# Expert weight sums: 64 jobs spread over three stages instead of two, with other buffers and other DMA rows

## The chip, the cores and the metric

The kernel runs on one core of a Trainium2 chip. The metric is the time of one execution on the device in microseconds (us): 1686.47 us before the change, the median of 3 runs (1685.59 to 1688.97). The engines are named as in the profile: PE (TensorE matmuls), PEld (its weight loads), DVE (VectorE), ACT (ScalarE), POOL (GpSimd) and SP (SyncE, whose queue issues almost all DMAs here).

## What is computed

The reference, cut to its three stages (S = 768, 2 batches, 8 heads of 64, 8 experts):

```
q_assign, k_assign = argmax of the normalised q, k against 16 centroids
scores = scale * q @ k.T, kept where q_assign == k_assign, else -1e9
x = softmax(scores) @ v                       # attention, 1536 x 512
h = x @ w_in; g = max(h, 0) + log1p(exp(-|h|))
x = g @ w_out                                 # first feed-forward stage, d_ff = 2048
P = softmax-like gate, 8 rounds of row and column normalisation
for e in range(8):
    out += P[:, e:e+1] * (relu(x @ w1[e]) @ w2[e])   # d_ff = 1024 per expert
```

## The kernel before

All matmuls take fp32 operands as two parts, a rounded one (names with h) and the rest (names with l), and make three products: h·h, h·l, l·h. A "split" is what makes the two: ACT casts, and POOL or DVE subtracts.

**Attention** (0 to 335 us): 8 head pairs, each of 4 halves of 6 steps, 192 steps in all. Scores go through line 478 (`s`), exponentials through ACT (`E`, line 491), transposes through PE (`t`, line 518), their split `eh`/`el` (lines 521 and 525), and the products with v through line 533 (`av`). All is put into a list of events with a step number, the list is sorted, and the pieces of code are recorded in that order; then a scheduler sets each engine's own order.

**First feed-forward stage** (335 to 656 us): 16 units (8 column blocks fc times 2 token blocks) of 48 first-layer matmuls (line 637, `p`) and 48 second-layer matmuls (`y`). The weights come as 64-bit numbers: `fetch_unit` loads them (SP, lines 133 and 137) and `to32` converts them on ACT and DVE (lines 117 to 121, `cm`, `wf`, `w2f`) once for two units; `split_unit` then splits them on ACT and POOL (lines 231 to 236, `wlA`, `wlBD`, `w2l`). The conversions of the next fc write `wf` (one buffer) and `w2f` (three tiles, two for each fc), which the splits of this fc read.

**Expert stage** (656 to 1685 us): 16 passes (8 experts times 2 token blocks) of 28 steps. Each pass multiplies 2 x 2 blocks with seven products instead of eight, so it needs sums of weight blocks, T1 to T4, of w1 and of w2. In a pass, 4 units u of 7 first-layer groups (line 887) use w1 parts A, B, C (`w1_load`, `w1_split`, lines 814 and 815: `whAm`, `wlAm`, `wlCm` and so on), and 14 second-layer pieces (line 922) use w2 parts (`w2_load`, line 835 and on, `w2_split`, lines 844 and 845: `vh`, `vl`; `vl` is made on POOL, three pieces ahead of its use). `vl` and `wlC` are POOL's whole work there.

**The weight sums** are made ahead of time, in 64 jobs (m = 0 for w1 or 1 for w2, expert e, quarter u):
- `t_load` (lines 188 and 191): SP loads 512 KB into a tile `ts`;
- `t_sums` (line 200): four subtractions 128x256 on POOL, in place;
- `t_store` (line 203): SP writes the tile's 512 KB into DRAM (`td`). `w1_load` (parts B and C) and `w2_load` read it from there in the expert stage.

A tile `ts` is free when its store has landed. The 32 w2 jobs run in attention with 3 tiles, the 32 w1 jobs in the first feed-forward stage with 2 tiles; the expert stage has none. The two loops that set when each part of a job is recorded:

```
t = 24 + 4.9 * n                # attention steps: load t, sums t + 6, store t + 12
divmod(int(3.2 * m) + o, 7)     # feed-forward slots (7 per unit): o = 0, 3, 5
```

Of the kernel before, what the change touches and what calls it, by code (L numbers as in the profile page):

```python
# [20 lines left out]
def attention_moe_moe2(ctx, tc, v, qt, kt, centroids, w_in, w_out, w_gate, w1, w2, eye, out, dbg=None):  # L21
# [139 lines left out]
    def fetch_unit(u):  # L161
# [11 lines left out]
            [lambda c=c: conv_half(w2f[c], r2, "2", c) for c in range(2)],  # L173
        )

    TD = [
        [[tc.dram_tile([P, 4, KC // 2 * P], F32, name=f"td{m}_{e}_{u}") for u in range(NF2)] for e in range(E)]
        for m in range(2)
    ]
    TS = {}  # L180
    TORD = (("T1", "T3", "T2", "T4"), ("T1", "T3", "T4", "T2"))

    def t_load(pool, m, e, u):
        t = TS[m, e, u] = slot_pool[pool].tile([P, 4, KC // 2 * P], F32, tag="ts", name=f"ts{m}_{e}_{u}", bufs=TSB[pool])
        for fh in range(2):
            o = fh * (FE // 2) + u * P
            if m:
                nc.sync.dma_start(t[:, 2 * fh : 2 * fh + 2, :].rearrange("p s d -> p (s d)"), w2[e, o : o + P, :])
            else:
                for j in range(2):  # L190
                    nc.sync.dma_start(
                        t[:, (0, 3, 1, 2)[2 * fh + j], :].rearrange("p (k f) -> p k f", f=P),
                        w1[e, j * DM // 2 : (j + 1) * DM // 2, o : o + P].rearrange("(k p) f -> p k f", p=P),
                    )

    def t_sums(m, e, u):
        t = TS[m, e, u]
        b11, b12, b22, b21 = (t[:, n, :] for n in ((0, 1, 3, 2) if m else (0, 1, 2, 3)))
        for o_, u_, v_ in ((b11, b12, b11), (b12, b22, b12), (b22, b22, b11), (b21, b21, b22)):
            nc.gpsimd.tensor_tensor(o_, u_, v_, ALU.subtract)  # L200

    def t_store(m, e, u):
        nc.sync.dma_start(TD[m][e][u], TS.pop((m, e, u)))

    TSB = {"ap": 3, "fp": 2}

    WT = {}

# [10 lines left out]
    def split_unit(u):  # L219
        nm = f"{u[0]}{u[1]}_{u[2]}_{u[3]}"  # L220
        par = u[3] % 2
        w2f = W[u]
        T = {"A": w1_tiles("A", par, nm), "D": w1_tiles("B", par, "D" + nm, "fp" if par else "mp")}
        w2h, w2l = (slot_pool["fp"].tile([P, 2, DM], F32R, tag=f"w2{t}{par}", name=f"w2{t}" + nm, bufs=1) for t in "hl")
        W[u] = w1_use(T), w2h, w2l

        def w1_(ch):
            h, l = T[ch]
            o = SLOT[MEMBERS[ch][0]]
            src = wf[:, o : o + 2, :]  # L230
# [348 lines left out]
        at(92 + (n - 1) * 1.36, lambda n=n: fetch_first(n), ("fu", 0))  # L579
    for n in range(4):  # L580
        at(175 + n * 5, lambda n=n: x_split("1_0", first_blk, n), ("xs", 0))
    for n in range(E * NF2):
        e, u = divmod(n, NF2)
        t = 24 + 4.9 * n
        at(t, lambda e=e, u=u: t_load("ap", 1, e, u), ("tl", 0))
        at(t + 6, lambda e=e, u=u: t_sums(1, e, u), ("tq", 0))
        at(t + 12, lambda e=e, u=u: t_store(1, e, u), ("tw", 0))
    KEEP = {'sp2': 1, 'fr': 0, 'av': 1, 'am3': 1, 'tpa': 1, 'smc': 0, 'm0': 1, 'rw': 1, 'pz': 1, 'e1': 1}
    events.sort(key=lambda x: x[:2])
    last_prep = max(key for key, _, fn, _ in events if fn in prep_fns)  # L590
# [194 lines left out]
    def w1_load(k, u, ch):  # L785
        e = k % E
        if ch == "A" and u % 2 == 0:
            for c_, b_ in CHUNK.items():
                WR[0, c_] = [wf[:, b_ : b_ + (3 if c_ == "C" else 2), :]]
        dst = WR[u % 2, ch]  # L790
        if ch == "A":
            nc.sync.dma_start(
                dst[0].rearrange("p s (k f) -> p (s k) f", f=P),
                w1[e, :, u * P : (u + 1) * P].rearrange("(k p) f -> p k f", p=P),
            )
        elif ch == "B":
            nc.sync.dma_start(dst[0], TD[0][e][u][:, 0:4:2, :])
        else:
            o = FE // 2 + u * P
            b22 = dst[0][:, 0, :]  # L800
            nc.sync.dma_start(
                b22.rearrange("p (k f) -> p k f", f=P),
                w1[e, DM // 2 : DM, o : o + P].rearrange("(k p) f -> p k f", p=P),
            )
            nc.sync.dma_start(dst[0][:, 1:3, :] if len(dst) == 1 else dst[1], TD[0][e][u][:, 1:4:2, :])

    def w1_split(k, u, ch):
        par = u % 2 if ch == "A" else 0
        h, l = T = w1_tiles(ch, par, f"m{k}_{u}")
        n = 0  # L810
        for src in WR[u % 2, ch]:
            m = src.shape[1]
            hs = h[:, n : n + m, :]
            nc.scalar.copy(hs, src)  # L814
            (nc.gpsimd if ch == "C" else nc.vector).tensor_tensor(l[:, n : n + m, :], src, hs.bitcast(F32), ALU.subtract)
            n += m
        W1U.setdefault((k, u), {}).update(w1_use({ch: T}))

# [22 lines left out]
    def w2_split(k, i, p):
        src = W2R[(7 * k + i) % 4][:, 2 * p : 2 * p + 2, :]
# [139 lines left out]
    for k in range(NB):  # L982
# [123 lines left out]
```

## Time and profile before

| what | value |
|---|---|
| median of 3 runs | 1686.47 us (1685.59 to 1688.97) |
| the profiled execution | 1686.74 us, its span 1684.9 us |
| mean granted TensorE clock, share of full speed | 0.961 |
| busy: PE, PEld, DVE, ACT, POOL | 1556.9, 1472.5, 1266.4, 1006.4, 830.8 us |
| sums `ts` on POOL (line 200) | 256 instructions, 203.5 us busy, 798 ns each |
| splits `vl` on POOL (line 845) | 224 instructions, 356.9 us busy, 1594 ns each |
| store of a job, from issue to landing, median | 3.1 us (512 KB) |

The busy times are sums over stages that have different limits, so the stage is what to look at first, and within it the waits and the timelines. A group of rows below is cited by its number. In a row of waits the engine and line on the left waited for what stands on the right. A time in square brackets in a timeline is the idle time ahead of the row, and what ended it.

### The profile page before, as it was taken

The page shows a single profiled execution, that of the slowest core. Times are in us where ns is not written, and L with a number is a line of the kernel's source. Part 1 is how long each engine was busy: PE and PEld are TensorE (multiplying, and loading weights), DVE is VectorE, ACT ScalarE, POOL GpSimd, SP SyncE. Part 2 cuts the span into 40 slices and gives each one's busy share as a digit, 9 for nine tenths or more (in the row PEclk, how much of TensorE's full clock was granted, in tenths as well). Part 3 has the DMA queues.
Part 4 walks back from the last instruction along what each step waited for, and adds up shares of the span by engine and source line. Part 5 has one row for each costly group of instructions (what it writes and reads, how often), then busy time and mean ns, then how long its engine had stood idle before and what let it go on. Part 6 is the DMA issues. An engine that isn't in the chain of part 4 may idle for free. (4 is left out here: it accounts for less than half of the span.)

```text
span 1684.9 us, 27842 instructions
## 1 busy us (share of the span) xinstructions
PE 1556.9 (92%) x9873; PEld 1472.5 (87%) x9873; DVE 1266.4 (75%) x1835; ACT 1006.4 (60%) x1854; POOL 830.8 (49%) x728
## 2 busy tenths in 40 slices
PE   5888898779777998999999999998999999999998
PEld 4777777668777997789999999998999999999998
DVE  4997877696555636697788787889687878877867
ACT  4777777655444554555666656656566656666654
POOL 3465656586555412234554445446444444544444
PEclk7989989899979999999999999999999999999999
DMA  8667877367666410233333444343534343443321
GB/s 219 174 188 218 235 241 217 129 185 230 213 200 194 147 32 26 91 99 118 119 120 117 125 127 125 112 124 94 166 118 125 113 126 123 122 124 118 121 72 65
DMA packets 228090, 236.30 MB, mean 140 GB/s; under 512 B 16880, under 2 KB 199280, under 8 KB 227952
## 3 DMA queue, kind: packets, MB, share of 16 engines
q1 hardware_dynamic: 227808, 234.47, 45.5%
q8 instruction: 77, 1.26, 0.3%
q14 instruction: 61, 0.50, 0.1%
q10 hardware_dynamic: 144, 0.07, 0.0%
HBM read 177.32 MB, written 36.70 MB: 127 GB/s over the span
## 5 line engine op out<-in xcount | busy, mean ns | idle before, releaser
L845 POOL TENSOR_TENSOR vl<-w2r,vh 128x512 fp32r<-128x512 f32 x224 | 356.9, 1594 | 459.1 <-ACT vh L844 413.9
L200 POOL TENSOR_TENSOR ts<-ts 128x256 f32<-128x256 f32 x256 | 203.5, 798 | 113.9 <-DMA ts<-in_moe_w_dram 83.6
L866 DVE TENSOR_TENSOR gl<-XA,gh 128x768 fp32r<-128x768 f32 x160 | 168.1, 1051 | 86.3 <-ACT gh L865 86.3
L865 ACT CAST gh<-XA 128x768 fp32r<-128x768 f32 x160 | 133.9, 837 | 114.6 <-PE Ya1m L922 97.6
L922 PE MATMUL Ya0m<-vh,gl 128*128 128x256 f32 x512 | 144.7, 283 | 0.0
L922 PE MATMUL Ya0m<-vl,gh 128*128 128x256 f32 x512 | 144.6, 282 | 0.0
L922 PE MATMUL Ya0m<-vh,gh 128*128 128x256 f32 x512 | 144.5, 282 | 0.0
L844 ACT CAST vh<-w2r 128x512 fp32r<-128x512 f32 x224 | 137.6, 615 | 9.2 <-PE y L671 5.9
L525 DVE TENSOR_TENSOR el<-t,eh 128x384 fp32r<-128x384 f32 x192 | 102.4, 551 | 33.4 <-ACT eh L521 32.3
L486 DVE TENSOR_REDUCE sc<-s 128x1 f32<-128x768 f32 x96 | 91.3, 952 | 28.4 <-PE s L478 27.8
L922 PE MATMUL Yb0m<-vl,gh 128*128 128x256 f32 x384 | 109.6, 285 | 2.5 <-POOL vl L845 2.5
L922 PE MATMUL Yb0m<-vh,gh 128*128 128x256 f32 x384 | 109.3, 285 | 2.3 <-DVE x L940 2.3
L922 PE MATMUL Yb0m<-vh,gl 128*128 128x256 f32 x384 | 109.7, 286 | 1.9 <-DVE gl L866 1.9
L521 ACT CAST eh<-t 128x384 fp32r<-128x384 f32 x192 | 90.0, 481 | 34.5 <-PE t L518 28.6
L518 PE MATMUL t<-idf,E 128*128 128x128 f32 x576 | 103.7, 293 | 6.9 <-ACT E L491 3.3
L491 ACT ACTIVATE E<-s,sc 128x768 f32<-128x768 f32 x96 | 86.9, 905 | 30.9 <-DVE sc L486 27.2
L908 ACT ACTIVATE XA<-XA 128x768 f32<-128x768 f32 x96 | 81.1, 844 | 28.8 <-DVE XA L906 28.7
L922 PEld LDWEIGHTS Ya0m<-vh,gl 128*128 128x128 f32 x512 | 97.5, 190 | 0.0
L922 PEld LDWEIGHTS Ya0m<-vh,gh 128*128 128x128 f32 x512 | 97.4, 190 | 0.0
L922 PEld LDWEIGHTS Ya0m<-vl,gh 128*128 128x128 f32 x512 | 97.3, 190 | 0.0
L518 PEld LDWEIGHTS t<-idf,E 128*128 128x128 f32 x576 | 78.0, 151 | 19.1 <-DVE el L525 7.5
L860 DVE TENSOR_TENSOR XS<-XA,XA 128x768 f32<-128x768 f32 x32 | 64.6, 2020 | 33.6 <-ACT XA L904 33.6
(243 smaller groups left out, 5334.2 us busy)
## 6 DMA issues: line engine op xcount, KB each, us to landing
td<-ts SPq DMA_DIRECT2D x64, 512.0 KB, 3.1
w2r<-td SPq DMA_DIRECT2D x256, 128.0 KB, 2.5
w2r<-in_moe_w_dram SPq DMA_DIRECT2D x48, 512.0 KB, 3.7
ts<-in_moe_w_dram SPq DMA_DIRECT2D x64, 256.0 KB, 4.4
ts<-in_moe_w_dram SPq DMA_DIRECT2D x128, 128.0 KB, 3.7
wf<-td SPq DMA_DIRECT2D x64, 256.0 KB, 3.2
w1r<-td SPq DMA_DIRECT2D x64, 256.0 KB, 3.1
AT<-HL SPq DMA_DIRECT2D x64, 192.0 KB, 5.3
```

Of the source, the lines that this page charges most:

```text
L200: nc.gpsimd.tensor_tensor(o_, u_, v_, ALU.subtract)
L486: nc.vector.tensor_reduce(SC[i][:, 0, j, t : t + 1], Et[i, t][:, :, 0:CB], AX.XY, ALU.max, negate=True)
L491: nc.scalar.activation(e.rearrange("p (a c) -> p a c", a=2), Et[i, t][:, :, 0:CB], AF.Exp, bias=sc[:, 0, j, t : t + 1], scale=1.0, accum_o ...
L518: nc.tensor.transpose(pt[:, t * P : (t + 1) * P], Et[i, t][:, s * P : (s + 1) * P], idf)
L521: nc.scalar.copy(eh, TT[i, s])
L525: nc.vector.tensor_tensor(el, TT.pop((i, s)), EHL[i, s].bitcast(F32), ALU.subtract)
L844: nc.scalar.copy(h, src)
L845: nc.gpsimd.tensor_tensor(l, src, h.bitcast(F32), ALU.subtract)
L865: nc.scalar.copy(h, src)
L866: nc.vector.tensor_tensor(l, src, h.bitcast(F32), ALU.subtract)
L908: nc.scalar.activation(t, t, AF.Relu)
L922: nc.tensor.matmul(ps, g[:, v, ts], w[:, v, :], start=i in (0, 1, 3) and p == 0 and v == 0 and n == 0 and t != 1, stop=p == 1 and v == 1 a ...
```

## The change

The same 64 jobs are made in another order (by expert: w1 then w2 of expert 0, and so on) and in three places: 16 jobs (experts 0 and 1) in attention, one each 10 steps, with load, sums and store 0, 8 and 17 steps after its start, 3 tiles; 24 (experts 2 to 4) in the first feed-forward stage, one each 3.9 slots, 0, 5 and 10 slots, 4 tiles; 24 (experts 5 to 7) in the expert stage, recorded one each 7 steps, at 0, 3 and 5.5 steps, with 1 tile. A job is cut in another way for w1 (128 rows of the matrix and 512 of its columns), so its loads are 2 DMAs of 256 KB in rows of 1 KB (4 of 128 KB in rows of 512 B before), and for w2 they are 2 of 256 KB in rows of 2 KB. Stores write rows of 1 KB (4 KB before), as one DMA of 512 KB (w2) or two of 256 KB (w1). A w2 part of sums now comes back with one DMA of 512 KB (4 of 128 KB), the sums in parts B and C of w1 in rows of 512 B (1 KB). Part A of w1 has one pair of tiles in the expert stage instead of two; in the feed-forward stage the odd pair moves to another pool. Every sum, split and matmul is there as often as before.

```diff
     TD = [
-        [[tc.dram_tile([P, 4, KC // 2 * P], F32, name=f"td{m}_{e}_{u}") for u in range(NF2)] for e in range(E)]
-        for m in range(2)
+        [tc.dram_tile([4, 2, P, HF], F32, name=f"td0_{e}") for e in range(E)],
+        [tc.dram_tile([4, NF2, P, DM // 2], F32, name=f"td1_{e}") for e in range(E)],
     ]
     def t_load(pool, m, e, u):
...
+        for h in range(2):
             if m:
-                nc.sync.dma_start(t[:, 2 * fh : 2 * fh + 2, :].rearrange("p s d -> p (s d)"), w2[e, o : o + P, :])
+                o = h * HF + u * P
+                src, d = w2[e, o : o + P, :].rearrange("p (s d) -> p s d", s=2), t[:, 2 * h : 2 * h + 2, :]
             else:
-                for j in range(2):
-                    nc.sync.dma_start(
-                        t[:, (0, 3, 1, 2)[2 * fh + j], :].rearrange("p (k f) -> p k f", f=P),
-                        w1[e, j * DM // 2 : (j + 1) * DM // 2, o : o + P].rearrange("(k p) f -> p k f", p=P),
-                    )
+                k, c = divmod(u, 2)
+                o = h * DM // 2 + k * P
+                src = w1[e, o : o + P, :].rearrange("p (s f) -> p s f", s=2)[:, :, c * 256 : (c + 1) * 256]
+                d = t[:, 2 * h : 2 * h + 2, :]
+            nc.sync.dma_start(d, src)
     def t_store(m, e, u):
-        nc.sync.dma_start(TD[m][e][u], TS.pop((m, e, u)))
-
-    TSB = {"ap": 3, "fp": 2}
+        t = TS.pop((m, e, u))
+        if m:
+            nc.sync.dma_start(TD[1][e][:, u].rearrange("s p d -> p s d"), t)
+            return
...
+        for n, ts_ in enumerate((t[:, 0:4:3, :], t[:, 1:3, :])):
+            nc.sync.dma_start(TD[0][e][2 * n : 2 * n + 2, k, :, cs].rearrange("s p f -> p s f"), ts_)
+
+    TSB = {"ap": 3, "fp": 4, "gp": 1}
+    JOBS = [(m, e, u) for e in range(E) for m in range(2) for u in range(NF2)]
+    JA, JF = 4 * NF2, 10 * NF2
-        T = {"A": w1_tiles("A", par, nm), "D": w1_tiles("B", par, "D" + nm, "fp" if par else "mp")}
+        pool = "fp" if par else "mp"
+        T = {"A": w1_tiles("A", par, nm, pool), "D": w1_tiles("B", par, "D" + nm, pool)}
-    for n in range(E * NF2):
-        e, u = divmod(n, NF2)
-        t = 24 + 4.9 * n
-        at(t, lambda e=e, u=u: t_load("ap", 1, e, u), ("tl", 0))
-        at(t + 6, lambda e=e, u=u: t_sums(1, e, u), ("tq", 0))
-        at(t + 12, lambda e=e, u=u: t_store(1, e, u), ("tw", 0))
+    for n, job in enumerate(JOBS[:JA]):
+        t = 22 + 10 * n
+        for o, fn, c_ in ((0, t_load, "tl"), (8, t_sums, "tq"), (17, t_store, "tw")):
+            at(t + o, lambda fn=fn, job=job: fn(*((("ap",) if fn is t_load else ()) + job)), (c_, 0))
     def w1_split(k, u, ch):
-        par = u % 2 if ch == "A" else 0
-        h, l = T = w1_tiles(ch, par, f"m{k}_{u}")
+        h, l = T = w1_tiles(ch, 0, f"m{k}_{u}")
     def w2_load(k, i):
...
-            n = TORD[1].index(name)
-            for u in range(NF2):
-                nc.sync.dma_start(dst[:, u, :], TD[1][e][u][:, n, :])
+            nc.sync.dma_start(dst, TD[1][e][TORD.index(name)].rearrange("u p d -> p u d"))
+    for n, job in enumerate(JOBS[JF:]):
+        t = G1 + 7 * n + 1.5
+        do(t, t_load, "gp", *job)
+        do(t + 3, t_sums, *job)
+        do(t + 5.5, t_store, *job)
-    for m in range(E * NF2):
-        e, u = divmod(m, NF2)
-        for o, fn in ((0, lambda e=e, u=u: t_load("fp", 0, e, u)), (3, lambda e=e, u=u: t_sums(0, e, u)),
-                      (5, lambda e=e, u=u: t_store(0, e, u))):
-            tsum_at.setdefault(divmod(int(3.2 * m) + o, 7), []).append(fn)
+    for n, job in enumerate(JOBS[JA:JF]):
+        for o, fn in ((0, lambda job=job: t_load("fp", *job)), (5, lambda job=job: t_sums(*job)),
+                      (10, lambda job=job: t_store(*job))):
+            tsum_at.setdefault(divmod(int(3.9 * n) + o, 7), []).append(fn)
```

Three places show what this does to the order. The line numbers of the change are some 11 to 16 higher than before (478 becomes 489, 518 becomes 529, 533 becomes 544).

PE in attention, third pair. Before, the score products of halves 10 and 11 (`s10_1` to `s11_1`, lines 478) stand in a row behind a transpose, with no transpose and no product with v between them:

```order
L518 MATMUL t8_5_1445<-idf_65,E8_2_1318 128x128
L478 MATMUL s10_1_1473<-AT210_736,AT200_690 128x384 x2
L478 MATMUL s10_1_1473<-Bt210_737,Bt200_691 128x384 x2
L478 MATMUL s10_2_1513<-AT210_736,AT200_690 128x384 x2
L478 MATMUL s10_2_1513<-Bt210_737,Bt200_691 128x384 x2
L478 MATMUL s11_0_1557<-AT211_741,AT201_695 128x384 x2
L478 MATMUL s11_0_1557<-Bt211_742,Bt201_696 128x384 x2
L478 MATMUL s11_1_1592<-AT211_741,AT201_695 128x384 x2
L478 MATMUL s11_1_1592<-Bt211_742,Bt201_696 128x384 x2
```

The change, at the same transpose:

```order
L529 MATMUL t8_5_1383<-idf_65,E8_2_1255 128x128
L544 MATMUL av8_1322<-eh8_3_1344,VV20_851 128x384
L489 MATMUL s10_1_1408<-AT210_688,AT200_642 128x384 x2
L544 MATMUL av8_1322<-el8_3_1346,VV20_851 128x384
L529 MATMUL t9_0_1398<-idf_65,E9_0_1290 128x128
L529 MATMUL t9_0_1398<-idf_65,E9_1_1331 128x128
L529 MATMUL t9_0_1398<-idf_65,E9_2_1374 128x128
L544 MATMUL av8_1322<-eh8_4_1360,VV20_851 128x384
L489 MATMUL s10_1_1408<-Bt210_689,Bt200_643 128x384
```

The scores are now one or two at a time between transposes and products with v. Such runs stand at four places before (at `s10_1`, `s14_1`, `s18_1`, `s22_1`), and the change has none of the four; a shorter one at `s6_2` is in both.

SP in the first feed-forward stage (`ts0_2_2` is the tile of w1, expert 2, quarter 2; `td` its store, `r110` and `r210` raw weights). Before, two loads, then the two stores of the same jobs:

```order
L191 DMA ts0_2_2_5067<-in_moe2_w1_dram 128x2x128 x4
L191 DMA ts0_2_3_5146<-in_moe2_w1_dram 128x2x128 x4
L133 DMA r110_0_4_5306<-in_moe_w_in_dram 128x4x128
L203 DMA td0_2_2_84<-ts0_2_2_5067 128x1024
L203 DMA td0_2_3_85<-ts0_2_3_5146 128x1024
L137 DMA r210_0_4_5307<-in_moe_w_out_dram 128x512
L191 DMA ts0_3_0_5203<-in_moe2_w1_dram 128x2x128 x4
L191 DMA ts0_3_1_5284<-in_moe2_w1_dram 128x2x128 x4
```

The change:

```order
L195 DMA ts0_3_0_4828<-in_moe2_w1_dram 128x2x256 x2
L206 DMA td1_2_84<-ts1_2_2_4630 128x4x256
L195 DMA ts0_3_1_4939<-in_moe2_w1_dram 128x2x256 x2
L206 DMA td1_2_84<-ts1_2_3_4715 128x4x256
L195 DMA ts0_3_2_5028<-in_moe2_w1_dram 128x2x256 x2
L211 DMA td0_3_77<-ts0_3_0_4828 128x2x256 x2
```

Each store is now preceded by the load of the job two places later.

POOL in the expert stage, passes 2 and 3 (`vl2_10` is the split of piece 1, half 0, in pass 2; `ts` the sums). Before, the same splits stand there without the sums. The change:

```order
L857 TENSOR_TENSOR vl2_00_8743<-w2r1_6919,vh2_00_8742 128x512
L857 TENSOR_TENSOR vl2_01_8798<-w2r1_6919,vh2_01_8797 128x512
L201 TENSOR_TENSOR ts0_7_1_10618<-ts0_7_1_10618 128x256 x4
L857 TENSOR_TENSOR vl2_10_8851<-w2r1_6919,vh2_10_8850 128x512
L829 TENSOR_TENSOR wlCm3_0_8899<-wf_71,whCm3_0_8898 128x768
L857 TENSOR_TENSOR vl2_11_8903<-w2r1_6919,vh2_11_8902 128x512
L201 TENSOR_TENSOR ts0_7_2_10801<-ts0_7_2_10801 128x256 x4
L857 TENSOR_TENSOR vl2_20_8956<-w2r0_6918,vh2_20_8955 128x512
```

All 24 jobs stand between the first splits of pass 0 and `wlCm3_3`, the last part of w1 in pass 3: some 7 in a pass, though they were recorded 4 in a pass.

## Rows read from the trace of the kernel before

**Rows 1.** Windows: us, PE, PEld, DVE, ACT, POOL busy, clock, DMA share, GB/s.
```profile
0.00:335.00 335.00, 274.43 (x1555) 237.42 (x1556) 254.20 (x453) 226.21 (x493) 183.79 (x243) 0.90 0.69 203
335.00:572.00 237.00, 194.79 (x1006) 179.35 (x1006) 156.35 (x223) 116.63 (x232) 145.60 (x154) 0.90 0.64 201
...
797.00:1100.00 303.00, 303.00 (x2098) 299.59 (x2097) 241.44 (x313) 190.03 (x320) 148.33 (x100) 1.00 0.39 121
```

**Rows 2.** Windows, matmuls of line 637 alone: us, PE, PEld busy, clock, DMA, GB/s.
```profile
347.10:554.50 207.40, 94.24 (x432) 83.88 (x433) 0.88 0.67 209
414.30:432.70 18.40, 9.26 (x49) 8.15 (x49) 1.00 0.84 256
371.50:392.20 20.70, 10.44 (x49) 9.31 (x50) 0.92 0.69 213
...
572.40:655.90 83.50, 45.30 (x240) 40.93 (x240) 1.00 0.14 43
```

**Rows 3.** Waits of SP's queue, 340 to 560 us: total us, times, longest.
```profile
SPq L203 <- POOL ts L200: 92.9, 28, 6.4
```

**Rows 4.** Waits of the other engines, 380 to 560 us, same columns.
```profile
POOL ts L200 <- DMA ts<-in_moe_w_dram: 55.1, 12, 8.4
...
PE p L637 <- DVE gf L651: 29.9, 10, 7.0
...
DVE w2f L119 <- POOL w2l L236: 19.8, 3, 8.9
```

**Rows 5.** Timeline of SP's queue: start, us, operation; no wait is in brackets here.
```profile
435.18 3.77 SPq L203 DMA_DIRECT2D td<-ts  x2
439.00 0.43 SPq L133 DMA_DIRECT2D r<-in_moe_w_in_dram  x1
439.47 4.64 SPq L191 DMA_DIRECT2D ts<-in_moe_w_dram  x8
```

**Rows 6.** Timeline of POOL: start, us, operation, idle before and releaser.
```profile
431.76 6.82 POOL L200 TENSOR_TENSOR ts<-ts 128x256 f32<-128x256 f32 x8 [7.04 <-DMA ts<-in_moe_w_dram]
...
445.20 6.88 POOL L200 TENSOR_TENSOR ts<-ts 128x256 f32<-128x256 f32 x8 [4.12 <-issue]
...
459.72 3.15 POOL L200 TENSOR_TENSOR ts<-ts 128x256 f32<-128x256 f32 x4 [6.38 <-DMA ts<-in_moe_w_dram]
```

**Rows 7.** Timeline of PE in attention, at the run of scores `s10_1`.
```profile
111.53 0.62 PE L478 MATMUL s<-AT,AT 128*128 128x384 f32 x2 [1.03 <-ACT E L491]
...
112.94 0.62 PE L478 MATMUL s<-AT,AT 128*128 128x384 f32 x2 [0.43 <-ACT E L491]
...
114.58 0.62 PE L478 MATMUL s<-AT,AT 128*128 128x384 f32 x2 [0.68 <-ACT E L491]
...
117.56 0.69 PE L533 MATMUL av<-el,VV 128*128 128x384 f32 x1 [1.40 <-DVE el L525]
```

**Rows 8.** Waits of PE, 264 to 331 us, end of attention.
```profile
PE rb L512 <- POOL rw L49: 6.1, 2, 4.5
```

**Rows 9.** Timeline of POOL in the expert stage.
```profile
678.13 2.50 POOL L845 TENSOR_TENSOR vl<-w2r,vh 128x512 fp32r<-128x512 f32 x2 [2.56 <-ACT vh L844]
...
832.51 1.99 POOL L815 TENSOR_TENSOR wlCm<-w1r,whCm 128x256 fp32r<-128x256 f32 x2
...
893.21 1.99 POOL L815 TENSOR_TENSOR wlCm<-w1r,whCm 128x256 fp32r<-128x256 f32 x2
```

**Rows 10.** DMA issues in attention, 0 to 335 us: count, KB, median us to landing.
```profile
ts<-in_moe_w_dram SPq DMA_DIRECT2D x64, 256.0 KB, 4.4
td<-ts SPq DMA_DIRECT2D x32, 512.0 KB, 4.1
```

**Rows 11.** DMA issues in the feed-forward stage, 380 to 560 us.
```profile
td<-ts SPq DMA_DIRECT2D x25, 512.0 KB, 3.0
```

**Rows 12.** DMA issues in the expert stage, 800 to 1100 us.
```profile
w1r<-in_moe_w_dram SPq DMA_DIRECT2D x10, 256.0 KB, 3.8
wf<-in_moe_w_dram SPq DMA_DIRECT2D x10, 256.0 KB, 2.8
```

More of the change, by code (lines that the diff above doesn't have):

```diff
@@ L174, in fetch_unit @@
         )
+    HF = FE // 2
     TD = [
-        [[tc.dram_tile([P, 4, KC // 2 * P], F32, name=f"td{m}_{e}_{u}") for u in range(NF2)] for e in range(E)]
-        for m in range(2)
+        [tc.dram_tile([4, 2, P, HF], F32, name=f"td0_{e}") for e in range(E)],
+        [tc.dram_tile([4, NF2, P, DM // 2], F32, name=f"td1_{e}") for e in range(E)],
     ]
     TS = {}
-    TORD = (("T1", "T3", "T2", "T4"), ("T1", "T3", "T4", "T2"))
+    TORD = ("T1", "T3", "T4", "T2")
     def t_load(pool, m, e, u):
-        t = TS[m, e, u] = slot_pool[pool].tile([P, 4, KC // 2 * P], F32, tag="ts", name=f"ts{m}_{e}_{u}", bufs=TSB[pool])
-        for fh in range(2):
-            o = fh * (FE // 2) + u * P
+        t = TS[m, e, u] = slot_pool[pool].tile([P, 4, 256], F32, tag="ts", name=f"ts{m}_{e}_{u}", bufs=TSB[pool])
+        for h in range(2):
             if m:
-                nc.sync.dma_start(t[:, 2 * fh : 2 * fh + 2, :].rearrange("p s d -> p (s d)"), w2[e, o : o + P, :])
-            else:
-                for j in range(2):
-                    nc.sync.dma_start(
-                        t[:, (0, 3, 1, 2)[2 * fh + j], :].rearrange("p (k f) -> p k f", f=P),
-                        w1[e, j * DM // 2 : (j + 1) * DM // 2, o : o + P].rearrange("(k p) f -> p k f", p=P),
-                    )
+                o = h * HF + u * P
+                src, d = w2[e, o : o + P, :].rearrange("p (s d) -> p s d", s=2), t[:, 2 * h : 2 * h + 2, :]
+            else:
+                k, c = divmod(u, 2)
[3 more added lines that the diff above has]
+            nc.sync.dma_start(d, src)
     def t_sums(m, e, u):
         t = TS[m, e, u]
-        b11, b12, b22, b21 = (t[:, n, :] for n in ((0, 1, 3, 2) if m else (0, 1, 2, 3)))
+        b11, b12, b21, b22 = (t[:, n, :] for n in range(4))
         for o_, u_, v_ in ((b11, b12, b11), (b12, b22, b12), (b22, b22, b11), (b21, b21, b22)):
@@ L202, in t_store @@
     def t_store(m, e, u):
-        nc.sync.dma_start(TD[m][e][u], TS.pop((m, e, u)))
-    TSB = {"ap": 3, "fp": 2}
+        t = TS.pop((m, e, u))
+        if m:
+            nc.sync.dma_start(TD[1][e][:, u].rearrange("s p d -> p s d"), t)
+            return
+        k, c = divmod(u, 2)
+        cs = slice(c * 256, (c + 1) * 256)
+        for n, ts_ in enumerate((t[:, 0:4:3, :], t[:, 1:3, :])):
[3 more added lines that the diff above has]
+    JA, JF = 4 * NF2, 10 * NF2
     WT = {}
@@ L796, in w1_load @@
         elif ch == "B":
-            nc.sync.dma_start(dst[0], TD[0][e][u][:, 0:4:2, :])
+            nc.sync.dma_start(
+                dst[0].rearrange("p s (k f) -> p (s k) f", f=P),
+                TD[0][e][0:2, :, :, u * P : (u + 1) * P].rearrange("s k p f -> p (s k) f"),
+            )
         else:
@@ L804, in w1_load @@
             )
-            nc.sync.dma_start(dst[0][:, 1:3, :] if len(dst) == 1 else dst[1], TD[0][e][u][:, 1:4:2, :])
+            nc.sync.dma_start(
+                (dst[0][:, 1:3, :] if len(dst) == 1 else dst[1]).rearrange("p s (k f) -> p (s k) f", f=P),
+                TD[0][e][2:4, :, :, u * P : (u + 1) * P].rearrange("s k p f -> p (s k) f"),
+            )
     def w1_split(k, u, ch):
-        par = u % 2 if ch == "A" else 0
-        h, l = T = w1_tiles(ch, par, f"m{k}_{u}")
+        h, l = T = w1_tiles(ch, 0, f"m{k}_{u}")
         n = 0
```

## The prediction, made before the change was timed

> **What bounds the kernel now.** I read the busy time by stage first, then the waits in the stage that has idle time, then timelines of the engines that those waits name.
>
> By stage [rows 1] PE is busy 303.00 of 303 us in the expert stage at clock 1.00, while POOL is busy 148.33: there PE's matmuls are the bound, and POOL has half its time to spare. A pass takes 60.7 us (the same POOL split is at 832.51 and at 893.21 [rows 9]). In attention PE is idle 335 - 274.43 = 60.6 us, in the first feed-forward stage 237 - 194.79 = 42.2 us, both at clock 0.90. What can be gained is there; what can be lost is in the expert stage, which has no idle PE time to give.
>
> In the feed-forward stage nine units take 207.40 us, 23.0 each, and the five at the end, beside which no sums are made, 83.50, 16.7 each [rows 2]. The reader is to see why the nine are slow. SP's queue stands 92.9 of 220 us at a store that waits for POOL's sums [rows 3]; POOL stands 55.1 us for the loads of sums, which are behind those stores on SP; DVE's conversions stand for POOL's splits, which are behind the sums, and PE stands 29.9 us for DVE [rows 4]. It is a ping-pong over two tiles: store of two jobs at 435.18 (held 3.77 us by the wait), then their loads at 439.47 [rows 5], then sums at 445.20, and from one pair of sums to the next 445.20 - 431.76 = 13.4 and 459.72 - 445.20 = 14.5 us [rows 6]. That is 7.0 us for a job of 3.2 us of sums. POOL's order puts 6 to 7.5 jobs between the weight splits of one fc and the next, that is two units: 6.6 x 7.0 = 46 us, and two units took 2 x 23.0 = 46.
>
> In attention a run of score matmuls on PE waits for the exponentials that free its PSUM tiles, while transposes and products with v that could go stand behind it: 1.03 + 0.43 + 0.68 + 1.40 = 3.5 us at the run of `s10_1` [rows 7]. At the end PE waits 6.1 us for `rw` on POOL, 4.5 in one piece [rows 8].
>
> **The change, part by part.** The terms go against the profiled execution, 1686.74 us, which is 0.27 us from the median of the runs.
>
> *Attention, 16 jobs instead of 32.* SP's stores and loads there halve, POOL loses 16 x 3.2 = 51 us, and the four long runs of scores go. I take 2.5 us for each run, since part of its waiting stays with the exponentials, and 6 for the wait at the end, ahead of which POOL's order now has no sums: 4 x 2.5 + 6 = **-16**. Bounds: -4 (only the piece of 4.5 us goes) and -20 (4 x 3.5 + 6). Late next is DVE, busy 254.20 of 335 us [rows 1]. The w1 jobs in this stage go through the same queue as the loads of q, k and v, which they now pass less often.
>
> *Feed-forward stage, 24 jobs with 4 tiles.* A load now goes ahead of the store two jobs earlier, so SP no longer holds the next load behind POOL. One job's round is 4.4 (load [rows 10]) + 3.2 + 3.0 (store [rows 11]) + 0.4 to issue (439.00 [rows 5]) = 11 us; over four tiles 2.8 us a job. The order has 7 jobs for two units: POOL needs 7 x 3.2 + about 5 of splits = 28 us, less than two units. DMA: 7 jobs x 1 MB and 4 raw loads of 512 KB make 9.4 million bytes; over 36.8 us that is 256 GB/s, exactly what the unit at 414.30 moved at share 0.84 while taking 18.4 us [rows 2]. So I take 18.4 for a unit without the ping-pong. Eight of the nine units gain 23.0 - 18.4 (the first, where DVE converts two sets, I leave out): **-37**. Bounds: -18, if they become like the unit at 371.50 with 20.7, and -50, if like the last five with 16.7. All 24 jobs are done about where the 32 were, so nothing more is late behind them.
>
> *Expert stage, 24 jobs with 1 tile.* No row of before shows sums here. With one tile a job is a chain: sums, store lands, load is issued and lands, next sums. Sums 3.2 (3.15 at 459.72 [rows 6]), store 3.0 [rows 11], issue 0.4, load 3.8 [rows 12], and the splits that POOL's order puts between the four sums of a job, 14 in all of 1 to 2 us each [rows 9], 0.8 a job: 11.2 us. POOL runs in order. The first sums follow the first splits of pass 0 (678.13) and the last stand in `wlCm3_3` (893.21 [rows 9]): the 23 steps between had 214 us, 9.3 each. So POOL falls behind by 23 x (11.2 - 9.3) = 44. `vl` is three of a pass's 14 pieces ahead, 3 x 60.7 / 14 = 13.0, less 3 for cast and split: some 10 us can be lost before PE waits. 44 - 10 = 34, and with the clock that PE may lose in such waits (0.90 in the two stages where it waits [rows 1]) **+35**. Bounds: 0 for a chain of 9.4 (load 2.8 [rows 12], no splits within), and +73 for one of 12.9 (landings as in attention, 4.1 and 4.4 [rows 10]). I take the landings of the feed-forward and expert rows since the expert stage moves 121 GB/s, against 203 in attention [rows 1]. SP waits for the sums and for the store to land; behind it are the reloads of w1 and w2. Those of w1 are recorded over 7 steps, some 15 us, ahead of their split, longer than one wait of SP (under 7 us by the chain), so they come in time.
>
> The Trainium skill bears on this chain: "DMA: Bandwidth & Descriptors", section "Anatomy of one DMA — SWDGE (gpsimd) path", fits a DMA as 2.0 us and 436 KB a microsecond, most of the 2.0 being the wait until the last byte is confirmed. By it, as an estimate, a 512 KB store is 3.2 and a 256 KB load 2.6 us; these DMAs go by SP's queue, and the rows have 3.0 to 4.1 and 2.8 to 4.4. The chain by the page would be 3.2 + 3.2 + 0.4 + 2.6 + 0.8 = 10.2 us, the term 23 x 0.9 - 10 = +11 and the total 1645 us.
>
> *The rest, at nothing.* One 512 KB reload of w2 for four of 128 KB: it lands perhaps a microsecond later, under the 10 us lead of `vl`. Sums in w1's parts B and C come in rows of 512 B: the two rows of that size are 3.8 and 2.8 [rows 12], under the lead of 15 us. One pair of A tiles: A is read by the first two of a unit's seven groups, so it is free five groups, some 11 us, before the next unit starts, and its cast now waits at the place where the cast for the unit after stood. Without those covers each would cost a few us per pass.
>
> Sum: 1686.74 - 16 - 37 + 35 = 1668.7, **1669 us**.
>
> **Rivals.**
> 1. *The single tile costs more than the other stages give (slower).* The chain with loaded landings is 12.9 us, since the stage now also moves 24 MB of sums: 23 x 3.6 - 10 = +73, in total 1686.74 - 53 + 73 = **1707**. It decides from the point where the term is 53, that is 9.3 + 63 / 23 = 12.0 us a job. For it: each of load, store and sums is on the chain and may only get longer, and a POOL sum beside DVE has been up to 0.86 (6.88 / 8 [rows 6]). Against it: the expert stage's DMA share of 0.39 [rows 1].
> 2. *The lead takes it all.* With a chain of at most 9.7 us (9.3 + 10 / 23) POOL never makes PE wait: 1686.74 - 53 = **1634**. For it: a load of 2.8 [rows 12]. Against it: nothing may stand in between, and 14 splits do.
> 3. *The feed-forward stage has another bound.* Conversions on ACT and DVE keep a unit at 20.7 as at 371.50 [rows 2], though POOL and SP are free: 8 x 2.3 = -18 and in total **1688**, as before; so the change does not do what it says. For it: DVE there is busy 156.35 of 237 us [rows 1], and the page of the profile shows no unit below 18 with jobs beside it but one. Against it: the waits of DVE in [rows 4] are for POOL.
>
> **How the numbers follow.** Forecast 0.48 (1652 to 1683); rival 1 0.24 (1687 to 1730); rival 2 0.13 (1625 to 1650); rival 3 0.15 (1682 to 1694). What can be told from no change is 0.2%, 3.4 us: 1683.1 to 1689.9. Faster: 0.48 + 0.13 and 0.02 of rival 3, 0.63. Same: 0.08 of rival 3 and of rival 1's edge. Slower: 0.29. The range is 1640 to 1710: it holds the forecast, rival 3, half of rival 1 and a third of rival 2, 0.80 together. The forecast's own range is 1652 to 1683.
>
> **What would show it.** Right: units of 18 to 19 us up to the fifth fc, SP's waits on sums there gone; no run of scores with PE idle at `s10_1`; in the expert stage 24 sums 11 us apart, POOL waiting for the load of `ts`, and PE waiting for `vl` in passes 1 to 3 for some 35 us, none after. Wrong: sums 12 us or more apart; or units that stay above 20 us; or PE without waits in passes 1 to 3.

## The result and the profile after

The change is slower: 1700.77 us median (1699.01 to 1703.77, 4 runs) against 1687.08 (1685.59 to 1688.97, 4 runs), a ratio of 1.0082 with a 95% interval of 1.0064 to 1.0100. The forecast was 1669 us and faster by over 0.2%; the time lies in the range (1640 to 1710), but in the part that belongs to the first rival (1707), whose sign came true.

The profiled execution of the change has a span of 1702.0 us, 17.1 more than before. Three events split it: the first feed-forward unit starts at 315.2 instead of 334.8 (-19.6), the first first-layer group of the expert stage at 636.4 instead of 675.8, so the feed-forward stage takes 321.2 instead of 341.0 (-19.8), and from there to the end it takes 1065.6 instead of 1009.1 (+56.5). The forecast's terms were -16, -37 and +35. So attention came out near the forecast's size, the feed-forward stage gave half, and the expert stage cost over half as much again.

The windows of the change by stage (columns as in [rows 1]): attention, the expert stage while sums are made in it, and three passes after.

```profile
0.00:315.00 315.00, 261.20 (x1554) 232.73 (x1554) 252.06 (x452) 225.13 (x492) 138.17 (x179) 0.91 0.59 164
```
```profile
636.40:925.00 288.60, 239.95 (x1472) 225.98 (x1471) 188.15 (x285) 137.47 (x235) 188.94 (x164) 0.93 0.57 175
925.00:1107.00 182.00, 182.00 (x1262) 179.95 (x1261) 145.85 (x189) 114.02 (x193) 88.91 (x60) 1.00 0.41 124
```

The same 1472 matmuls that take 288.6 us here took 231.1 before (this window of before, from the first group to the same place):

```profile
675.80:906.90 231.10, 224.37 (x1471) 213.64 (x1470) 180.20 (x284) 136.88 (x234) 97.12 (x66) 0.99 0.36 112
```

Of the 57.5 us between them 15.6 are matmuls that ran longer (239.95 against 224.37 busy, the granted clock at 0.93 against 0.99), and 41.9 are idle time of PE. After pass 3 all is as before: 182.00 us for three passes at clock 1.00, with one pair of A tiles and reloads in rows of 512 B. So these two parts of the change cost nothing there, as forecast.

The waits of the change in the expert stage, 640 to 915 us (engine line <- what it waited for: us, times, longest): first of POOL and PE, then of SP's queue.

```profile
POOL ts L201 <- DMA ts<-in_moe_w_dram: 90.2, 31, 6.9
...
PE l0m L899 <- POOL wlCm L829: 36.5, 12, 4.8
```
```profile
SPq L195 <- DMA td<-ts: 40.6, 20, 4.6
SPq L206 <- POOL ts L201: 34.3, 11, 3.6
SPq L211 <- POOL ts L201: 27.8, 20, 2.9
```

That is the chain of the prediction, link by link: SP waits for the sums to store them, then for the store to land, POOL waits for the load, and PE for a split that is queued behind. POOL's timeline shows one turn of it, the wait for the load and then a job's sums among the splits:

```profile
806.26 0.80 POOL L201 TENSOR_TENSOR ts<-ts 128x256 f32<-128x256 f32 x1 [4.85 <-DMA ts<-in_moe_w_dram]
807.01 2.00 POOL L857 TENSOR_TENSOR vl<-w2r,vh 128x512 fp32r<-128x512 f32 x1
808.97 3.97 POOL L201 TENSOR_TENSOR ts<-ts 128x256 f32<-128x256 f32 x3
812.90 1.80 POOL L829 TENSOR_TENSOR wlCm<-wf,whCm 128x768 fp32r<-128x768 f32 x1
814.66 2.52 POOL L857 TENSOR_TENSOR vl<-w2r,vh 128x512 fp32r<-128x512 f32 x2
```

The 24 jobs start their sums from 640.1 to 912.5, 23 steps of 11.84 us. What PE waits for is not `vl`, as the prediction had it (1.5 us from 640 to 925), but `wlC` (40.4 us in the same time), the last part of w1 in a unit, which is split in the unit that uses it.

In the feed-forward stage (matmuls of line 646, columns as in [rows 2]) the units with sums are as slow as before, but they are six and not nine:

```profile
327.50:466.00 138.50, 63.71 (x289) 56.95 (x290) 0.90 0.72 237
466.00:599.40 133.40, 72.01 (x384) 65.43 (x385) 1.00 0.18 57
```

138.5 / 6 = 23.1 us a unit, where [rows 2] had 23.0; then 133.4 / 8 = 16.7. SP's waits there show where the stall went: 92.9 us in 220 for sums [rows 3] have become 13.4 in 138 (328 to 466 us), and the raw weights' loads, which waited 10.2 us in the 220 before, wait 58.5 for the conversions:

```profile
SPq L137 <- DVE w2f L121: 43.0, 5, 12.9
...
SPq L133 <- DVE wf L121: 15.5, 3, 7.4
SPq L211 <- POOL ts L201: 7.9, 13, 2.3
SPq L206 <- POOL ts L201: 5.5, 4, 2.4
```

PE still waits for DVE, and DVE's conversions for POOL's splits, as in [rows 4]:

```profile
PE p L646 <- DVE gf L660: 23.1, 9, 4.4
...
DVE wf L119 <- POOL wlBD L243: 10.9, 2, 7.3
```

SP's timeline has nothing between 377.73 and 386.72, and the loads of the next sums stand behind:

```profile
377.25 0.48 SPq L133 DMA_DIRECT2D r<-in_moe_w_in_dram  x1
386.72 0.34 SPq L137 DMA_DIRECT2D r<-in_moe_w_out_dram  x1
...
388.13 1.20 SPq L195 DMA_DIRECT2D ts<-in_moe_w_dram  x2
```

In attention the run of scores at `s10_1` is gone as the order said, and so is the wait for `rw` [rows 8]: from 244 to 312 us PE's longest wait is another, 3.0 us.

```profile
PE po L431 <- POOL OH L424: 3.0, 1, 3.0
```

### The profile page after: what moved, and what is told of

It is laid out like the page before. It is cut to its first block, busy times and chain, and to the rows that moved or that the text cites. A ratio compares the mean times of both kernels' runs of the same rounds, so it can differ in the third digit from the quotient of the medians.

```text
span 1702.0 us, 27339 instructions
## 1 busy us (share of the span) xinstructions
PE 1552.5 (91%) x9873; PEld 1474.4 (87%) x9873; DVE 1277.2 (75%) x1835; ACT 1007.3 (59%) x1854; POOL 852.2 (50%) x728
## 5 line engine op out<-in xcount | busy, mean ns | idle before, releaser
L201 POOL TENSOR_TENSOR ts<-ts 128x256 f32<-128x256 f32 x256 | 228.0, 894 | 123.5 <-DMA ts<-in_moe_w_dram 109.7
L878 DVE TENSOR_TENSOR gl<-XA,gh 128x768 fp32r<-128x768 f32 x160 | 172.9, 1082 | 86.7 <-ACT gh L877 86.5
L497 DVE TENSOR_REDUCE sc<-s 128x1 f32<-128x768 f32 x96 | 91.1, 950 | 25.9 <-PE s L489 25.6
L877 ACT CAST gh<-XS 128x768 fp32r<-128x768 f32 x64 | 53.4, 836 | 58.4 <-PE Yb1m L934 44.2
```

What stands on the lines that cost most here:

```text
L497: nc.vector.tensor_reduce(SC[i][:, 0, j, t : t + 1], Et[i, t][:, :, 0:CB], AX.XY, ALU.max, negate=True)
L878: nc.vector.tensor_tensor(l, src, h.bitcast(F32), ALU.subtract)
```

## The experiments

Two causes could stand behind the expert stage's +57 us and the units that stayed slow. **Packing**: sums are dear where the scheduler puts them closer together than their round takes, since POOL works in order and the splits that PE needs stand behind them. **Amount**: each job costs some time through POOL, DVE and the DMAs, 57 / 24 = 2.4 us in the expert stage and 1.6 in the feed-forward stage, wherever it stands. The first three runs keep all jobs, tiles and stages and change the order alone.

### Holding the sums at their recorded place

```diff
+    def held(fn, *args):
+        with ExitStack() as es:
+            for ins in last_of_engines(("Pool",)):
+                es.enter_context(tc.issue_after(ins))
+            fn(*args)
...
-        do(t + 3, t_sums, *job)
+        do(t + 3, held, t_sums, *job)
```

This is the run moe_held; in ffn_held `held(t_sums, *job)` stands in the feed-forward loop instead, in both_held in both.

> The changed kernel with one thing held: in the expert stage the sums of a job may not be put ahead of the last POOL instruction recorded before them, so that one job stands in each unit (7 steps, 15.2 us) and not seven in a pass of four units. Theory (packing): PE lost its 57 us there since POOL, in order, waited in each of the 23 steps for a chain of 11.8 us that had 9.3; at 15.2 us a job the chain always fits, the passes 0 to 3 take 58 to 63 us as before the change, and the time is 1644 us (1640 to 1655). Rival (amount): the sums cost PE time by their mere number, 57 / 24 = 2.4 us a job through POOL, DVE and the DMAs; then the loss is only spread over six passes and the time stays at 1695 to 1701.

Measured: 1654.67 us (1651.37 to 1656.34), ratio to the kernel before 0.9805 (0.9785 to 0.9826), at the upper end of what packing gave. Packing; amount is refuted. From the first group to the end of the span it is 1016.9 us (1651.8 - 634.9), where before had 1009.1 and the change 1065.6: all 24 jobs now cost 8 us instead of 57. The window of the same matmuls as above takes 234.8 us, and PE no longer waits for POOL at all:

```profile
634.90:869.70 234.80, 224.86 (x1475) 214.46 (x1474) 188.88 (x288) 137.51 (x237) 151.60 (x116) 0.99 0.52 160
869.70:1055.80 186.10, 181.54 (x1257) 179.66 (x1258) 155.83 (x189) 112.58 (x191) 141.93 (x109) 1.00 0.61 186
```

What is left is 1.5 us a pass: 62.2 against 60.7 us, in the first unit of each pass with sums (PE `l3m` behind DVE `XA`). These 8 us are most of why the gain is 46 and not 57. A second tile in this stage, the other way to shorten a job's round, was not tried.

> The changed kernel with one thing held: in the feed-forward stage the sums of a job may not be put ahead of the last POOL instruction recorded before them, so that 3 to 4 jobs and not 8 or 9 stand between the weight splits of one fc and the next. Theory (packing): the six units of 23.1 us were slow since 8 to 9 jobs of 5.1 us had to go through POOL ahead of the splits that the next conversions wait for; with 4 jobs (20 us and 5 of splits in 33) nothing waits, units take 17 to 18.5 us all along, and the time falls by 20 to 34 us to 1667 to 1681. Rival (amount): each job costs PE (23.1 - 16.7) x 6 / 24 = 1.6 us wherever it stands; units take 19.5 to 20.5 over thirteen units, and the time stays at 1696 to 1702.

Measured: 1683.89 us (1679.84 to 1690.19), ratio 0.9984 (0.9968 to 1.0000), so 17 us less than the change: just above packing's range and far under amount's. Packing, though the split is another than expected: the first three units stay slow, 68.5 us or 22.8 each, and all later ones take 184.1 / 11 = 16.7, ten of them with 16 jobs beside them, as if there were none. The count in the expectation was off, too: in the change's trace five to seven jobs, not eight or nine, stand on POOL between the `w2l` splits of one fc and of the next; here it is two to four.

```profile
326.20:394.70 68.50, 31.86 (x145) 28.54 (x146) 0.88 0.61 204
394.70:578.80 184.10, 99.24 (x528) 89.98 (x529) 1.00 0.45 144
```

> Both of the above. Theory (packing): the two gains add up, 1700.8 - 57 - 27 = 1617 us (1608 to 1635), less than the kernel before and the change. Rival (amount): 1690 to 1702.

Measured: 1634.28 us (1634.17 to 1636.35), ratio 0.969 (0.9672 to 0.9707). The two gains add up (46 + 17 = 63; 1700.77 - 1634.28 = 66), at the upper end of what packing gave. This kernel is faster than both.

### The DMA shapes alone

The kernel before with the change's `t_load`, `t_sums`, `t_store` and reloads; the jobs as before.

```diff
-            for u in range(NF2):
-                nc.sync.dma_start(dst[:, u, :], TD[1][e][u][:, n, :])
+            nc.sync.dma_start(dst, TD[1][e][TORD.index(name)].rearrange("u p d -> p u d"))
...
```

> The kernel before with the change's DMA shapes alone: jobs cut as in the change, loads of 2 x 256 KB, stores in rows of 1 KB, reloads of w2 sums in one DMA, of w1 sums in rows of 512 B. Jobs stay where they were: 32 in attention, 32 in the feed-forward stage with 2 tiles, none in the expert stage. Theory (the prediction's: shapes cost nothing, they are all covered): 1687 us, within 4. Rival: the rows change landings enough to matter to the ping-pong over two tiles, whose round holds two landings: 16 rounds by 1 us, so up to 16 us to either side.

Measured: 1685.41 us (1681.38 to 1687.45), ratio 0.9989 (0.9976 to 1.0003). No difference that this interval can tell: the larger loads, the smaller rows of the stores and the single reload are covered, as forecast.

### Attention alone

```diff
-    for n in range(E * NF2):
+    for n in range(E * NF2 // 2):
         e, u = divmod(n, NF2)
-        t = 24 + 4.9 * n
+        t = 22 + 10 * n
...
```

> The kernel before with the change's attention part alone: 16 of the 32 w2 jobs, one each 10 steps at 0, 8 and 17; the other 16 are left out (the sums of w2 of experts 4 to 7 are neither made nor stored, those of experts 0 to 3 are read in their place). Feed-forward and expert stage as before. Theory (fewer jobs let the scores lie among the other matmuls): -16 by the prediction's sum, -19.6 by the start of the first unit in the changed kernel (315.2 against 334.8), so 1666 to 1672 us and a first unit at 314 to 319. Rival (attention gained by something else in the change, rows or the order of the jobs): 1684 to 1688.

Measured: 1668.78 us (1666.23 to 1670.38), ratio 0.9879 (0.9861 to 0.9897); the first unit starts at 317.0. The gain comes with the number and spacing of jobs in attention, and it is kept to the end.

```profile
0.00:317.00 317.00, 259.84 (x1555) 232.12 (x1555) 253.72 (x453) 225.50 (x493) 138.25 (x179) 0.91 0.58 162
```

### Four tiles alone, and the raw loads on another queue

```diff
-    TSB = {"ap": 3, "fp": 2}
+    TSB = {"ap": 3, "fp": 4}
```

> The kernel before with 4 tiles instead of 2 for the sums of the feed-forward stage, nothing else. Theory of the prediction (the ping-pong over two tiles is what slows a unit, without it 18.4 us): 8 units by 4.6 us, about -37, 1650 us. Theory since (packing: four tiles shorten a job from 7.0 to 5.1 us, as in the changed kernel, but the scheduler puts correspondingly more jobs ahead of the next splits): units with jobs stay at 22 to 24 us, the jobs are done after 32 x 5.1 = 163 us or 7 units instead of 9 to 10, so 2 to 3 units by 6.4 us, 1668 to 1675 us.

Measured: 1666.79 us (1666.11 to 1668.67), ratio 0.987 (0.9853 to 0.9887): -22, just under packing's range and far from the -37 of the prediction. Ten units take 206.3 us, 20.6 each, from 16.7 to 25.9, and then four 16.7:

```profile
349.40:555.70 206.30, 98.79 (x481) 88.19 (x482) 0.94 0.71 225
555.70:622.40 66.70, 36.05 (x192) 32.73 (x193) 1.00 0.17 50
```

So four tiles do help, by 2.4 us a unit rather than 4.6, and neither theory had the way: units with jobs did get faster, against the packing theory, by half of what the prediction took, and the jobs were done after ten units, not seven.

In the changed kernel the raw loads were the queue's new wait. The run raw_on_act issues them elsewhere:

```diff
-            nc.sync.dma_start(
+            (nc.scalar if fc > 1 else nc.sync).dma_start(
...
```

> The changed kernel with the raw 64-bit weights of fc 2 to 7 issued from ACT's queue and not from SP's. In the changed kernel SP waits 59 us of 138 for DVE's conversions to free the raw tiles, with loads of sums behind. Theory (that wait has taken the place of the store's): the loads come sooner, POOL goes at 4 to 4.5 us a job, the 24 jobs end one unit earlier, 5 slow units of 22 to 23 us: -5 to -12, 1689 to 1696 us, and POOL waits for loads less than 8 us instead of 16.2. Rival (POOL's own work and the splits behind 8 to 9 jobs set the unit whatever SP does): 1698 to 1703.

Measured: 1698.93 us (1697.49 to 1701.06), ratio 1.006 (1.0042 to 1.0078); against the change's 1700.77 no difference of weight. The wait on SP did go, POOL's sums wait for no load, and the jobs end one unit sooner, but the five units take 118.2 / 5 = 23.6 us. POOL (327 to 466 us of the change, 326 to 445 us of this run: count, busy, mean ns, idle before):

```profile
L201 POOL TENSOR_TENSOR ts<-ts 128x256 f32<-128x256 f32 x93 | 83.6, 905 | 21.1 <-DMA ts<-in_moe_w_dram 16.2
```
```profile
L201 POOL TENSOR_TENSOR ts<-ts 128x256 f32<-128x256 f32 x93 | 84.5, 917 | 5.1
```

So the wait on SP that had taken the store's place was not the bound either. With it gone, POOL's sums and splits fill 104 of 118 us (84.5 and 20 of splits), and the `w2l` splits of an fc still stand behind six to nine jobs. What the traces with four tiles have in common is that a unit's time goes with the jobs beside it: 16.7 us with 1.6 jobs a unit (ffn_held, its later units), 20.6 with 3.1 (four_tiles), 23.1 with 3.8 (the change) and 23.6 with 4.6 (this run). The cost of a job is so not a fixed amount: at 1.6 a unit it is nothing.

### A better place for the jobs

both_held still had three slow units at the start, beside the conversions of two fc. The run both_held_late starts the jobs later:

```diff
-            tsum_at.setdefault(divmod(int(3.9 * n) + o, 7), []).append(fn)
+            tsum_at.setdefault(divmod(int(3.2 * n) + 17 + o, 7), []).append(fn)
```

> Sums held in both stages as in the run both_held (1634.3 us), and the jobs of the feed-forward stage start 17 slots (2.4 units) later, one each 3.2 slots instead of 3.9. There units 1 to 3 were still slow (26.0, 21.7 and 20.7 us against 16.7). Theory (the sums beside the first units, where DVE is busiest, cost those 18 us): unit 1 at 21 to 24, units 2 and 3 at 17 to 18.5, with 4.4 jobs in two units later on nothing lost: -8 to -13, 1621 to 1627 us. Rival (the conversions of the first units and the splits of x alone make them slow): 1631 to 1638.

Measured: 1627.51 us (1624.62 to 1629.31), ratio 0.963 (0.961 to 0.9651), the fastest kernel of this study. The time is just above the expected 1621 to 1627, and so is one of the three units: they take 21.1, 18.6 and 17.9 us, 57.6 instead of 68.5:

```profile
327.30:384.90 57.60, 29.23 (x145) 25.93 (x146) 0.97 0.43 140
384.90:571.20 186.30, 99.45 (x528) 89.97 (x529) 1.00 0.53 174
```

Half of the 10.9 us is not from DVE's conversions: in these units of both_held (326 to 394 us) PE waited 6.4 us for POOL's `clA`, a split of x, which stood behind seven sums (323.17 to 330.49 us); here (327 to 385 us) it waits 0.8.

Three runs looked for the 1.5 us a pass that moe_held left. late_phase records the expert stage's sums at `t + 4.5` instead of `t + 3`:

> both_held_late (1627.5 us) with the sums of the expert stage recorded 1.5 steps later in their unit (4.5 instead of 3 steps after the load, store at 6.8). What is left there is 1.5 us in the first unit of each of six passes (16.7 against 15.2 us), where PE waits for DVE's XA. Theory (POOL's four sums fall beside DVE's work where DVE has none to spare in that unit, and both get slower): 1.5 steps later DVE is through, the units are 15.2 to 15.6, -6 to -9: 1618 to 1623 us. Rival (the sums slow DVE wherever they stand in that unit): within 3 of 1627.5.

Measured: 1635.54 us (1634.72 to 1637.07), slower by 8, which neither the theory nor the rival had. The first unit of a pass became 17.5 and the third 16.4 us, both with PE behind DVE's `XA`. late_spread records the four sums one by one, 0.8 steps apart:

> both_held_late (1627.5 us) with the four sums of a job in the expert stage recorded one by one, 0.8 steps apart, each held behind the POOL instruction before it. POOL's order then has three, a split, and the fourth. Theory (POOL beside a DVE without spare time): one sum of four moves away, a quarter to a half of the 1.5 us a pass goes: -2 to -5, 1622 to 1626. Rival: the amount of sums in that unit counts, not their place: within 2 of 1627.5.

Measured: 1632.78 us (1628.80 to 1632.83), 5 us slower and outside both ranges; the first unit stays at 16.7 and the third becomes 16.0 us. skip_first_unit leaves that unit free of sums:

```diff
-    JA, JF = 4 * NF2, 10 * NF2
+    JA, JF = 4 * NF2, 11 * NF2
...
-        t = G1 + 7 * n + 1.5
+        t = 28 * ((n + 1) // 3) + 7 * ((n + 1) % 3) + 8.5
-            tsum_at.setdefault(divmod(int(3.2 * n) + 17 + o, 7), []).append(fn)
+            tsum_at.setdefault(divmod(int(2.9 * n) + 14 + o, 7), []).append(fn)
```

> both_held_late with 28 jobs in the feed-forward stage (from slot 14, one each 2.9 slots, 4.8 in two units) and 20 in the expert stage, three a pass, none in the first unit of a pass. Theory (the first unit's DVE has no time to spare beside sums): all units of passes 1 to 6 at 15.2, -9; four more jobs in the feed-forward stage cost 0 to 4 while 4.8 jobs and the splits are 4.8 x 4 + 5 = 24 of 33 us: 1618 to 1624 us. Rival (sums cost some 0.4 us each wherever they stand): 1625 to 1632.

Measured: 1635.83 us (1632.63 to 1638.30). The first unit is still 16.7 us, with no sums recorded in it, and the four more jobs made one early feed-forward unit 23.9 us. So the theory that the sums in that unit slow DVE falls; passes without sums have the 1.5 us nowhere (60.7 us). The timelines show where they are. In that unit DVE does the same work in both kernels, but `gl` and the sum `XA<-XA,XA` take 2 us each instead of 1, and PE's `l3m` waits for what DVE does behind them. Here POOL's splits `vl` run beside them:

```profile
855.23 2.05 DVE L878 TENSOR_TENSOR gl<-XA,gh 128x768 fp32r<-128x768 f32 x1
857.20 2.04 DVE L872 TENSOR_TENSOR XA<-XA,XA 128x768 f32<-128x768 f32 x1
```
```profile
854.45 2.01 POOL L857 TENSOR_TENSOR vl<-w2r,vh 128x512 fp32r<-128x512 f32 x1
857.08 1.34 POOL L857 TENSOR_TENSOR vl<-w2r,vh 128x512 fp32r<-128x512 f32 x1 [0.62 <-ACT vh L856]
```

The same two in a pass of the changed kernel without sums, where POOL is idle when they start (989.76 to 991.71 us):

```profile
990.50 0.94 DVE L878 TENSOR_TENSOR gl<-XA,gh 128x768 fp32r<-128x768 f32 x1
991.37 0.95 DVE L872 TENSOR_TENSOR XA<-XA,XA 128x768 f32<-128x768 f32 x1
```

POOL had the sums of the last unit right ahead of those splits (845.72 to 850.71 us). That they push the splits beside DVE's work is the likely reading; no run tried that alone.

## Why the prediction was wrong, point by point

- **Attention, -16**: the two waits came out as forecast, the size in part by luck. It was -19.6 in the trace, and attention_16 alone gives 1 - 0.9879 of 1689 us, 20 us. PE's waits for exponentials fell by 9.0 us (10 in the sum) and the wait for `rw`, 6.1 us, went (6). But a wait that the sum did not have, for POOL's `OH`, rose from 2.4 to 13.7 us (attention_16 has the same three: 6.1, none and 14.9), so PE's idle time fell by only 6.8 us (60.6 to 53.8). The other 13.2 us are matmuls that ran shorter (274.43 us [rows 1] to 261.20), for which the sum had no term. Some 7 of them, as an estimate, come from the granted clock: in the traces it is at 1.2 GHz and not 2.4 for 68 us of the stage before and for 55 after, 43 fewer matmuls start at the lower level, and before the change one takes 489 ns there on average instead of 322. The rest is open. PE's waits before (0 to 334 us) and after (0 to 315 us):

```profile
PE s L478 <- ACT E L491: 15.6, 23, 1.3
...
PE po L420 <- POOL OH L413: 2.4, 2, 2.1
```
```profile
PE po L431 <- POOL OH L424: 13.7, 5, 3.4
...
PE s L489 <- ACT E L502: 6.6, 13, 1.3
```

- **Feed-forward stage, -37**: wrong step: "So I take 18.4 for a unit without the ping-pong." The unit at 414.30 that gave 18.4 was not one without the ping-pong but one with few sums in it. One more column of the window, which the prediction did not use, says so: POOL was busy 7.21 us in it, and 12.88 to 16.96 in the units around. In the change, with SP's waits for sums nearly gone, a unit with sums took 23.1 us.

```profile
392.20:414.30 22.10, 18.79 (x98) 17.13 (x97) 15.21 (x20) 11.88 (x24) 16.96 (x18) 0.92 0.63 209
414.30:432.70 18.40, 17.28 (x99) 15.65 (x97) 11.35 (x21) 8.90 (x18) 7.21 (x11) 1.00 0.84 256
432.70:456.80 24.10, 18.79 (x98) 17.49 (x97) 11.52 (x17) 12.53 (x25) 15.66 (x18) 0.86 0.71 227
```

  The other failing number is POOL's own work: "7 x 3.2 + about 5 of splits = 28 us". A sum took 905 ns there, not 800, and POOL was busy 101 us in 138.5, 34 in two units. What was gained is 24 jobs instead of 32 and 5.7 instead of 7.0 us a job (sums from 321.7 to 452.9 us, 23 steps), so three slow units fewer: 3 x (23.1 - 16.7) = 19, against 19.8 measured. The prediction had no term for fewer jobs: it gave its 4.6 us to eight units and took the 24 jobs to end about where the 32 had, but their last sums start 138 us after the stage's first unit, those of the 32 before 228.
- **Expert stage, +35**: the mechanism was right (a chain through one tile, POOL in order, PE behind it), two sizes were off. The job took 11.84 us, not 11.2, 23 x 0.64 = 15 us in all. The mean of the 23 steps in the trace is 3.85 of sums (962 ns each instead of 800; 3.2 in the sum), 1.35 of splits among them (0.8), 3.2 until the store has landed (3.0), 0.8 to issue the loads (0.4) and 2.6 from there to the next sums (3.8). So every term but the last was too short, by 1.8 us together, and the last 1.2 too long. (The 214 us of the prediction are 893.21 - 678.13 = 215.1; it makes 9.35 a step of 9.3 and changes nothing.)

```profile
L201 POOL TENSOR_TENSOR ts<-ts 128x256 f32<-128x256 f32 x92 | 88.5, 962 | 90.4 <-DMA ts<-in_moe_w_dram 84.6 <-issue 1.8
```

  And the lead of 10 us, "`vl` is three of a pass's 14 pieces ahead", was that of the wrong split. `wlC` is behind the same sums on POOL and is needed sooner: in the kernel before, its first product starts 6.0 to 7.7 us after the split ends (800 to 900 us). PE waited 40.4 us for it and 1.5 for `vl` (640 to 925 us). The POOL steps cost 23 x (11.84 - 9.3) = 58 us, and 57.5 arrived at PE. Nothing was absorbed.
- **The rest at nothing**: right, as far as shown (layout_only, and passes of 60.7 us after the jobs; what one pair of A tiles does while sums are made no run tests alone).
- **The rivals**: the first, "the single tile costs more than the other stages give", is the sign that came, though for another reason than its own: its landings of 4.1 and 4.4 us did not come (loads 3.2, stores 2.3 and 3.1 in the expert stage), and the job stayed under its point of 12.0 us. That point stood on the terms -16, -37 and a lead of 10. With the terms as measured, 19.6 + 19.8 = 39.4 us gained and no lead, it lies at 9.3 + 39.4 / 23 = 11.0 us.
- **The Trainium skill on DMAs**: by the Trainium skill, "DMA: Bandwidth & Descriptors", section "Anatomy of one DMA — SWDGE (gpsimd) path", the estimate was a chain of 10.2 us. Of its landings the store's 3.2 us agrees with the stage's median here (3.1 for 512 KB), the load's 2.6 is below it (3.2 for 256 KB). What the chain had beyond that is in the sums, the splits among them and the issue.

## What to carry to other kernels

Work that an in-order engine does in its idle time is nearly free only where its steps are further apart than their own round (8 us for 24 jobs in moe_held, 57 without the constraint). Where a scheduler sets the order, look at its order and not at the schedule that was recorded: here it put 7 jobs in a pass where 4 were written, and one constraint on the order was worth 66 us. When a lead is counted on to hide lateness, count it for every product that stands in the queue behind the late one, and take the shortest. When a row is taken as "this without that", read the other engines of the same stretch first.

## What was not expected of the hardware

POOL's sums got slower where DVE ran beside them, and DVE too. The sum 128x256 took 717 ns at its fastest, 829 ns on average in the feed-forward stage before (347 to 560 us), 905 after, and in moe_held, beside the expert stage's DVE, 1109 (807 to 1056 us). The 42 sums of the kernel before that had no DVE instruction beside them took 722 to 743 ns. In moe_held:

```profile
L201 POOL TENSOR_TENSOR ts<-ts 128x256 f32<-128x256 f32 x64 | 71.0, 1109 | 3.8
```

DVE's `gl` went in the same stretch to 1260 ns, where it had 1027 in the passes of the changed kernel without sums (925 to 1100 us); the 8 of the 40 that had no POOL instruction beside them took 945 to 948:

```profile
L878 DVE TENSOR_TENSOR gl<-XA,gh 128x768 fp32r<-128x768 f32 x40 | 50.4, 1260 | 20.4 <-ACT gh L877 20.4
```
```profile
L878 DVE TENSOR_TENSOR gl<-XA,gh 128x768 fp32r<-128x768 f32 x29 | 29.8, 1027 | 17.4 <-ACT gh L877 17.4
```

The Trainium skill has a rule for such pairs in "SBUF — State Buffer", section "Who interferes with whom": a DVE instruction with two inputs in SBUF, as `gl` is, contends with a GpSimd instruction that reads SBUF, over a pair of ports that the two share and that is locked while one uses it. The rows agree in sign; that it is the port, and not something else the two share, no run here shows.
